# Attention over grouped heads: output rows of four pairs regrouped by 0/1 matmuls before the store

## The chip, the cores and the metric

The kernel runs on one core of a Trainium2 chip. The metric is the device time of one execution in microseconds. A core has TensorE (PE, with its weight loads shown as PEld), VectorE (DVE), ScalarE (ACT), GpSimd (POOL) and SyncE (SP), each with its own instruction stream; they wait for one another by semaphores. SP issues all DMA transfers here, into one queue that the core's 16 DMA engines work off together: each transfer is split evenly over the 16, and its semaphore tells of its landing when all 16 are done.

## The reference

```python
B, Hq, Hkv, Sq, Sk, D = 16, 32, 8, 16, 2048, 128       # q, k, v in bf16
k = jnp.repeat(k, Hq // Hkv, axis=1)
v = jnp.repeat(v, Hq // Hkv, axis=1)
scores = jnp.einsum("bhqd,bhkd->bhqk", q, k) * D ** -0.5
p = softmax(scores, axis=-1)
return jnp.einsum("bhqk,bhkd->bhqd", p, v)
```

K and V are 67 MB each, q and the output 2.1 MB each.

## The kernel before, in words

Four query heads share one head of K and V: 4 x 16 = 64 query rows for each of 128 groups. Two groups make a *pair* (128 query rows), and the kernel goes through NP = 64 pairs. A pair loads 1 MB of K (`Kn`, 6 buffers, 8192 bytes in a row on each partition) and 1 MB of V (`Vb`, 8 buffers, rows of 4096 bytes). Q is loaded four pairs at once, a *chunk* of 128 KB whose partition a holds the four rows 4a to 4a+3 (`load_q`, L202): 1024 bytes in a row.

For pair p the engines do this:

- DVE transposes K in two halves (`kt`, L343, KT<-Kn), always two pairs ahead.
- PE multiplies Q with the transposed K in tiles of 32 rows and 64 columns (op "S", L274 and L233). The scores have one PSUM tensor, `S_ps`, so S(p+1) waits until DVE has read those of pair p.
- DVE scales the scores into `Sneg` and takes the row minimum of the negated scores (L361); later it takes 1/rowsum (`recip`, L352).
- ACT computes exp with the row sums (op "exp", L391), PE transposes P in two halves (op "PT", L285), ACT moves each half out of PSUM (op "pe", L401).
- PE multiplies with V (op "PV", L302) three steps later (PVLAG = 3), and ACT scales the result into one of eight buffers `Osb` in bf16 (op "norm", L411).
- POOL copies each chunk of Q four times side by side (L176), PE transposes it (op "QT", L252), and ACT moves that out (op "qe", L381), in two parts in the first two steps of a chunk.

The orders of PE and ACT are two lists written out ahead (`pe_prog`, `act_prog`, L93 to L142). Step p holds on PE: S(p+1), PV(p-3), PT(p), and QT in two of four steps; on ACT: exp(p), norm(p-3), the two "pe", and "qe". DVE's order in step p is Sneg(p), recip(p-1), kt(p+2). A PSUM bank (`ST_ps`, third bank) is kept for the Q transposes (`stage_ap`, L153). PE's list runs as a loop over eight pairs, with steps 4 to 59 in it; the others are written out in full.

SP's order is one loop over t (L215): load K(t); a chunk of Q where it is due; load V(t-5) (VLAG); store pair t-12 (SLAG). Each load waits for its buffer: K(t) for `kt` of pair t-6, V(p) for PV(p-8). The V of the last pair comes in three pieces (CUTS), so that its PV can start early. A pair's store (`store`, L210) waits for its norm and moves 32 KB, 256 bytes from each partition, in the order of the output's rows; norm(p) in turn waits for the store of pair p-8, whose buffer it uses.

At the start POOL makes an iota and two identity matrices (L167 to L170, `sem_id`), and PE waits for these (L230).

Of the kernel before, what the change touches and what calls it, by code (L numbers as in the profile page):

```python
# [6 lines left out]
ALU = mybir.AluOpType  # L7
# [12 lines left out]
VLAG = 5  # L20
PVLAG = 3
SLAG = 12
QLEAD = 7
CUTS = (0, 8, 13, 16)


def bass_standalone__gqa_softmax__sampling_kernel(
# [12 lines left out]
    J = Sk // 128  # L40
    assert J == 16 and NP % BODY == 0 and BODY % (2 * QPAIRS) == 0
    NQC = NP // QPAIRS
    scale = float(D) ** -0.5

    ctx = ExitStack()
# [16 lines left out]
    nbias = sb("nbias", [128, NP], F32)  # L62
    rowsum = sb("rowsum", [128, NP], F32)
    rrec = sb("rrec", [128, NP], F32)

    S_ps = ctx.enter_context(nc.psum_tensor("S_ps", [128, Sk], F32))
    ST_ps = ctx.enter_context(nc.psum_tensor("ST_ps", [128, 3 * 512], F32))
# [5 lines left out]
    sem_vl = [sem(f"sem_vl{i}") for i in range(len(CUTS) - 1)]  # L73
    sem_q = [sem(f"sem_q{i}") for i in range(NQ)]
    sem_o = [sem(f"sem_o{i}") for i in range(NO)]
    sem_kt = sem("sem_kt")
    sem_q4 = sem("sem_q4")
    sem_max = sem("sem_max")
# [17 lines left out]
    def stage(*what):  # L96
        stages.append(what)
        return len(stages) - 1
# [22 lines left out]
    for p in range(NP - 1):  # L121
        step_at[p] = len(pe_prog)
        pe_prog.append(("S", p + 1))
        act_prog.append(("exp", p))
        if p >= PVLAG:
            pv(p - PVLAG)
            norm(p - PVLAG)
        transposes(p)
        c, i = divmod(p, QPAIRS)
        if c + 1 < NQC and i < 2:  # L130
            q_part(c + 1, i)
    tail_at = len(pe_prog)
    for p in range(NP - 4, NP - 2):
        pv(p)
# [6 lines left out]
    pv(NP - 1)  # L141
    norm(NP - 1)  # L142
    last_q = {what[1:]: u for u, what in enumerate(stages) if what[0] == "Q"}
    last_p = {what[1:]: u for u, what in enumerate(stages) if what[0] == "P"}

    first = PVLAG + 1
# [16 lines left out]
    with nc.Block() as block:  # L163

        @block.gpsimd
        def _(gp):
            gp.iota(iota_t[:, :], [[1, 128]], base=0, channel_multiplier=-1).then_inc(sem_id, 1)  # L167
            gp.wait_ge(sem_id, 1)
            gp.tensor_scalar(ident[:, :], iota_t[:, :], 0.0, None, op0=ALU.is_equal).then_inc(sem_id, 1)
            gp.tensor_scalar(ident4[:, :], iota_t[:, :], 0.0, None, op0=ALU.is_equal).then_inc(sem_id, 1)  # L170
            for c in range(NQC):
                gp.wait_ge(sem_q[c % NQ], 16 * (c // NQ + 1))
                if c >= 1:
                    gp.wait_ge(sem_st, last_q[c - 1, 1] + 1)
                src = Qn[c % NQ][:, :, :].rearrange("p j (b x) -> p (j b) x", b=2)
                gp.tensor_copy(  # L176
                    Q4[:, :, :, :, :].rearrange("p j b r x -> p (j b) r x"),
                    src.unsqueeze(2).to_broadcast([128, 2 * QPAIRS, 4, 64]),
                ).then_inc(sem_q4, 1)

        @block.sync
        def _(sp):
            def load_k(p):
                s = p % NK
                if p >= NK:
                    sp.wait_ge(sem_kt, p - NK + 1)
                sp.dma_start(Kn[s][:, :], kf[p]).then_inc(sem_k[s], 16)  # L187

            def load_v(p):
                s = p % NV  # L190
                if p >= NV:
                    sp.wait_ge(sem_pv, p - NV + 1)
                if p < NP - 1:
                    dst = Vb[s][:, :, :, :].rearrange("a g j d -> a g (j d)")
                    sp.dma_start(dst, vf[:, 2 * p:2 * p + 2, :]).then_inc(sem_v[s], 16)  # L195
                    return
                for x, (lo, hi) in enumerate(zip(CUTS, CUTS[1:])):
                    dst = Vb[s][:, :, lo:hi, :].rearrange("a g j d -> a g (j d)")
                    src = vf[:, 2 * p:2 * p + 2, D * lo:D * hi]
                    sp.dma_start(dst, src).then_inc(sem_vl[x], 16)  # L200

            def load_q(c):  # L202
                s = c % NQ
                if c >= NQ:
                    sp.wait_ge(sem_q4, c - NQ + 1)
                rows = 128 * QPAIRS
                src = qf[rows * c:rows * (c + 1), :].rearrange("(a j) d -> a j d", j=QPAIRS)
                sp.dma_start(Qn[s][:, :, :], src).then_inc(sem_q[s], 16)

            def store(p):  # L210
                s = p % NO
                sp.wait_ge(sem_nm, p + 1)
                sp.dma_start(of[128 * p:128 * (p + 1), :], Osb[s][:, :]).then_inc(sem_o[s], 16)  # L213

            for t in range(NP + SLAG + 1):  # L215
# [12 lines left out]
        @block.tensor  # L228
        def _(pe):
            pe.wait_ge(sem_id, 3)  # L230

            def matmul_on_loaded(out, lhsT, rhs, tile, start, stop):
                return pe.add_instruction(mybir.InstMatmult(  # L233
# [7 lines left out]
            def emit(op, at, v_at):  # L241
# [36 lines left out]
                elif op[0] == "PT":  # L278
                    _, p, h, u = op
                    if h == 0:  # L280
                        pe.wait_ge(sem_exp, at(p + 1))
                    dst = stage_ap(("P", p, h))
                    for t in range(4):
                        x = 4 * h + t
                        ins = pe.transpose(dst[:, 128 * t:128 * (t + 1)], P[p % 2][:, 128 * x:128 * (x + 1)], ident4[:, :])  # L285
                    ins.then_inc(sem_st, 1)
                elif op[0] == "PV":
                    _, p = op
                    if p >= NP - 4:
                        pe.wait_ge(sem_ev, last_p[p, 1] + 1)  # L290
                    if p < NP - 1:
                        pe.wait_ge(sem_v[p % NV], v_at(p))
                    if p == NP - 3:
                        pe.wait_ge(sem_max, NP)
                    elif 1 <= p < NP - 3:
                        pe.wait_ge(sem_nm, at(p))
                    pt = PT[p % NPT][:, :, :].bitcast(BF16).rearrange("p t (q e) -> p t e q", e=2)
                    for j in range(J):
                        if p == NP - 1 and j in CUTS:
                            pe.wait_ge(sem_vl[CUTS.index(j)], 16)  # L300
                        for g in range(2):
                            ins = pe.matmul(  # L302
                                o_ap(p)[64 * g:64 * (g + 1), :],
                                pt[:, j // 2, j % 2, 64 * g:64 * (g + 1)],
                                Vb[p % NV][:, g, j, :],
                                start=(j == 0), stop=(j == J - 1),
                                skip_group_check=True,
                            )
                    ins.then_inc(sem_pv, 1)
# [64 lines left out]
        def _(act):  # L374
            for op in act_prog:
# [9 lines left out]
                elif op[0] == "exp":  # L385
                    _, p = op
                    act.wait_ge(sem_max, p + 1)
                    if p >= 2:
                        act.wait_ge(sem_st, last_p[p - 2, 1] + 1)

                    act.activation(  # L391
                        P[p % 2][:, :].bitcast(BF16).rearrange("p (n y e) -> p n y e", n=16, e=2),
                        Sneg[p % 2][:, :].rearrange("p (n e y) -> p n y e", n=16, e=2), ACT.Exp,
                        bias=nbias[:, p:p + 1], scale=-1.0, accum_out=rowsum[:, p:p + 1],
                    ).then_inc(sem_exp, 1)
                elif op[0] == "pe":
                    _, p, h, u = op
                    act.wait_ge(sem_st, u + 1)
                    if h == 0 and p >= NPT:
                        act.wait_ge(sem_pv, p - NPT + 1)  # L400
                    act.activation(  # L401
                        PT[p % NPT][:, 4 * h:4 * (h + 1), :].rearrange("p t q -> p (t q)"),
                        stage_ap(("P", p, h)), ACT.Copy,
                    ).then_inc(sem_ev, 1)
                else:
                    _, p = op
                    act.wait_ge(sem_pv, p + 1)
                    act.wait_ge(sem_rec, p + 1)
                    if p >= NO:
                        act.wait_ge(sem_o[p % NO], 16 * (p // NO))  # L410
                    act.activation(Osb[p % NO][:, :], o_ap(p), ACT.Copy,  # L411
                                   scale=rrec[:, p:p + 1]).then_inc(sem_nm, 1)

# [27 lines left out]
```

## Time and profile before

| | |
|---|---|
| median of three runs | 341.72 us (341.66 to 341.79) |
| profiled execution: whole / span on the core | 342.24 us / 340.5 us |
| granted TensorE clock, mean | 0.993 |
| read from HBM / written | 136.31 MB / 2.10 MB |
| mean rate over the span | 407 GB/s |
| DMA packets: all / under 512 B / under 2 KB | 38705 / 11552 / 14112 |
| Sneg (L361), 64 times | 2.26 us each |
| exp (L391), 64 times | 2.49 us each |
| half a K transpose (L343), 128 times | 1.22 us each |
| norm (L411), 61 times | 0.37 us each |

The span runs from the first instruction of the program to the last one on the core; the whole execution adds what lies around it. The profile counts an engine as busy when it works on data, not when it issues DMAs or waits. Under 512 bytes there are 8192 packets of 256 bytes (64 stores of 128 packets); nearly all others are the 4-byte packets that end a transfer on each of the 16 DMA engines. In the chain of work that ended last, "DMA Vb<-in_v_dram" is the time from issue to landing of a V load, its place in the queue included.

### The profile page before, as it was taken

Reading aid. Unit: us, or ns where it says so; the run is one execution under the profiler, and the core shown is the slowest. Engines: PE = TensorE matmul, PEld = TensorE weight load, DVE = VectorE, ACT = ScalarE, POOL = GpSimd, SP = SyncE. Lnnn points to the kernel's source line nnn. Section 1 sums busy time; section 2 is a strip of 40 time slices with the busy share of each in tenths; the row PEclk is TensorE's granted clock in tenths of the full one; section 3 lists DMA queues with packets and bytes.
Section 4 is the critical chain, followed back from the end, with each engine's and each line's share of the span. In section 5 each row is a group of like instructions: output and inputs, shape, how many; then the busy total and the mean of one; then the engine's idle time right before and its main releaser. Section 6 shows DMA issues by size and latency. Waiting matters only on the chain.

```text
span 340.5 us, 9888 instructions
## 1 busy us (share of the span) xinstructions
PE 278.8 (82%) x4736; PEld 161.6 (47%) x3712; DVE 295.3 (87%) x320; ACT 267.0 (78%) x353; POOL 31.8 (9%) x23
## 2 busy tenths in 40 slices
PE   0687999999998787888788797897878878888885
PEld 0233555555465445445355354454454454454454
DVE  2489999999999988989989889889889889899860
ACT  1178889999888786877878877887878869778785
POOL 3202020202010020200202011020200202000000
PEclk9979999999999999999999999999999999999999
DMA  8999999999999999999999999999999999999996
GB/s 295 398 418 416 410 414 409 414 415 415 416 418 415 416 417 417 415 419 417 416 418 412 420 418 413 420 416 417 420 413 418 414 416 420 419 415 420 416 409 205
DMA packets 38705, 138.63 MB, mean 407 GB/s; under 512 B 11552, under 2 KB 14112, under 8 KB 30496
## 3 DMA queue, kind: packets, MB, share of 16 engines
q1 hardware_dynamic: 38688, 138.43, 100.7%
q8 instruction: 8, 0.13, 0.2%
q14 instruction: 9, 0.07, 0.1%
HBM read 136.31 MB, written 2.10 MB: 407 GB/s over the span
## 4 chain that ended last, share of the span: by engine, by line
DMA 58%; DVE 16%; SPq 10%; issue 7%; PE 6%; ACT 1%; POOL 1%
DMA Vb<-in_v_dram 52%; DVE KT L343 11%; SPq L187 7%; DVE Sneg L361 5%; DMA Kn<-in_k_dram 5%; PE O_ps L302 3%; SPq L213 2%; DMA Qn<-in_q_dram 1%; ACT O L411 1%; PE S_ps L274 1%; PE S_ps L233 1%; SPq L195 1%; PE ST_ps L252 1%; POOL Q L176 1%; SPq L200 0%
## 5 line engine op out<-in xcount | busy, mean ns | idle before, releaser
L343 DVE STREAM_TRANSPOSE KT<-Kn 128x1024 f32<-128x1024 f32 x128 | 151.5, 1222 | 28.7 <-DMA Kn<-in_k_dram 28.7
L391 ACT ACTIVATE P<-Sneg,nbias 128x2048 bf16<-128x2048 f32 x64 | 159.6, 2493 | 6.0 <-DVE Sneg L361 6.0
L361 DVE TENSOR_SCALAR_CACHE_REDUCE Sneg<-S_ps 128x2048 f32<-128x2048 f32 x64 | 144.4, 2256 | 7.1 <-PE S_ps L233 7.1
L274 PE MATMUL S_ps<-KT,QT 32*64 32x512 bf16 x1024 | 105.7, 393 | 6.7 <-DVE Sneg L361 5.1
L233 PE MATMUL S_ps<-KT,QT 32*64 32x512 bf16 x1024 | 104.8, 388 | 0.0
L302 PE MATMUL O_ps<-Vb,PT 128*64 128x128 bf16 x1952 | 66.2, 221 | 38.0 <-DMA Vb<-in_v_dram 38.0
L302 PEld LDWEIGHTS O_ps<-Vb,PT 128*64 128x64 bf16 x1952 | 56.5, 110 | 80.4 <-issue 43.5
L401 ACT ACTIVATE PT<-ST_ps 128x512 f32<-128x512 f32 x128 | 69.5, 595 | 19.2 <-PE ST_ps L285 19.2
L285 PE MATMUL ST_ps<-ident,P 128*128 128x128 f32 x512 | 70.5, 281 | 4.7 <-ACT P L391 4.3
L274 PEld LDWEIGHTS S_ps<-KT,QT 32*64 32x64 bf16 x1024 | 32.4, 104 | 71.0 <-issue 60.3
L285 PEld LDWEIGHTS ST_ps<-ident,P 128*128 128x128 f32 x512 | 55.3, 141 | 13.9 <-ACT P L391 9.6
L176 POOL COPY Q<-Qn 128x2048 bf16<-128x2048 bf16 x16 | 30.3, 1893 | 255.9 <-PE ST_ps L252 252.0
L411 ACT ACTIVATE O<-O_ps,rrec 128x128 bf16<-128x128 f32 x61 | 22.5, 369 | 35.1 <-PE O_ps L302 35.0
L252 PE MATMUL ST_ps<-ident,Q 128*128 128x128 f32 x128 | 20.2, 282 | 8.8 <-POOL Q L176 8.1
L381 ACT ACTIVATE QT<-ST_ps 128x512 f32<-128x512 f32 x32 | 19.3, 603 | 8.5 <-PE ST_ps L252 8.5
L252 PEld LDWEIGHTS ST_ps<-ident,Q 128*128 128x128 f32 x128 | 15.5, 145 | 9.2 <-issue 8.1
L391 ACT ACTIVATION_READ_ACCUMULATOR P<-Sneg,nbias 128x1 f32 x64 | 13.2, 207 | 0.0
L352 DVE RECIPROCAL rrec<-rowsum 128x1 f32<-128x1 f32 x64 | 10.2, 159 | 3.0 <-ACT P L391 3.0
L361 DVE DVE_READ_ACCUMULATOR Sneg<-S_ps 128x1 f32 x64 | 5.3, 84 | 0.0
L302 PE MATMUL S_ps<-Vb,PT 128*64 128x128 bf16 x96 | 3.6, 221 | 1.1 <-issue 0.6
L302 PEld LDWEIGHTS S_ps<-Vb,PT 128*64 128x64 bf16 x96 | 2.9, 110 | 1.9 <-issue 1.5
L411 ACT ACTIVATE O<-S_ps,rrec 128x128 bf16<-128x128 f32 x3 | 1.1, 369 | 2.0 <-PE S_ps L302 2.0
(8 smaller groups left out, 3.0 us busy)
## 6 DMA issues: line engine op xcount, KB each, us to landing
Kn<-in_k_dram SPq DMA_DIRECT2D x64, 1024.0 KB, 15.9
Vb<-in_v_dram SPq DMA_DIRECT2D x63, 1024.0 KB, 16.4
Qn<-in_q_dram SPq DMA_DIRECT2D x16, 128.0 KB, 15.5
out_dram<-O SPq DMA_DIRECT2D x64, 32.0 KB, 15.4
Vb<-in_v_dram SPq DMA_DIRECT2D x1, 512.0 KB, 12.6
Vb<-in_v_dram SPq DMA_DIRECT2D x1, 320.0 KB, 12.3
Vb<-in_v_dram SPq DMA_DIRECT2D x1, 192.0 KB, 12.4
```

The lines of the kernel that those rows point to most:

```text
L176: gp.tensor_copy(Q4[:, :, :, :, :].rearrange("p j b r x -> p (j b) r x"), src.unsqueeze(2).to_broadcast([128, 2 * QPAIRS, 4, 64]),).then_i ...
L187: sp.dma_start(Kn[s][:, :], kf[p]).then_inc(sem_k[s], 16)
L233: return pe.add_instruction(mybir.InstMatmult(name=nc.get_next_instruction_name(), engine=mybir.EngineType.PE, ins=[pe.lower_ap(rhs), pe.l ...
L252: ins = pe.transpose(dst[:, 128 * j:128 * (j + 1)], src[:, j, b, :], ident4[:, :])
L274: ins = pe.matmul(s_ap, w, x, start=(acc == 0), stop=(acc == 3))
L285: ins = pe.transpose(dst[:, 128 * t:128 * (t + 1)], P[p % 2][:, 128 * x:128 * (x + 1)], ident4[:, :])
L302: ins = pe.matmul(o_ap(p)[64 * g:64 * (g + 1), :], pt[:, j // 2, j % 2, 64 * g:64 * (g + 1)], Vb[p % NV][:, g, j, :], start=(j == 0), stop ...
L343: ins = dve.transpose(KT[p % NKT][:, :].rearrange("p (t b e a x) -> p x e t b a", t=J // 2, b=2, e=2, x=2)[:, x, :, :, :, :], Kn[p % NK][: ...
L361: dve.tensor_scalar(Sneg[p % 2][:, :].rearrange("p (t h x) -> p h t x", t=8, h=2), S_ps[:, :].rearrange("p (h t x) -> p h t x", t=8, h=2), ...
L391: act.activation(P[p % 2][:, :].bitcast(BF16).rearrange("p (n y e) -> p n y e", n=16, e=2), Sneg[p % 2][:, :].rearrange("p (n e y) -> p n ...
L401: act.activation(PT[p % NPT][:, 4 * h:4 * (h + 1), :].rearrange("p t q -> p (t q)"), stage_ap(("P", p, h)), ACT.Copy,).then_inc(sem_ev, 1)
L411: act.activation(Osb[p % NO][:, :], o_ap(p), ACT.Copy, scale=rrec[:, p:p + 1]).then_inc(sem_nm, 1)
```

## The change

The outputs of pairs 0 to 55 are no longer stored pair by pair. Four pairs make a chunk, as with Q; there are NRC = 14 such chunks, and the last eight pairs keep the store that they had.

- A constant `sel` of 0 and 1 is made by POOL with a further iota and a compare: sel[p, j, a] is 1 where p = 4a + j. PE's first wait, and so everything on PE, is now for these as well (`sem_id` 5 in place of 3).
- A new PE op "R" for chunk c, placed at the end of step p = 4c + 7 (RLAG = 7), multiplies for each pair x of the chunk and each j the `Osb` of that pair by sel[:, j, :]: 16 matmuls with 128 x 32 weights and 128 columns. Row 4a + j of pair x comes to partition 32x + a, columns 128j to 128j + 127. The result fills the PSUM bank that the Q transposes use.
- A new ACT op "re", at the end of the same step, moves the 128 x 512 values out of PSUM into one of four buffers `Rsb` in bf16. From chunk 4 on it waits for the store of four chunks before.
- SP stores chunk c at t = 4c + 18 (RSLAG = 18): 128 KB, 1024 bytes from each partition, which are one run of the output. It waits for "re". The pair's own store remains for pairs 56 to 63, at t = p + 12 as before.
- norm no longer waits for an earlier store of its buffer.

`sel` and `Rsb` are allocated after all other buffers in SBUF, so that these keep their places.

```diff
+RLAG = 7
+RSLAG = 18
+NR = 4
...
+    NRC = NP // QPAIRS - 2
...
+    sel = sb("sel", [128, QPAIRS, 32], BF16)
+    Rsb = [sb(f"R{i}", [128, QPAIRS, 128], BF16) for i in range(NR)]
...
             q_part(c + 1, i)
+        c, i = divmod(p - RLAG, QPAIRS)
+        if i == 0 and 0 <= c < NRC:
+            u = stage("R", c)
+            pe_prog.append(("R", c))
+            act_prog.append(("re", c, u))
...
+            gp.wait_ge(sem_id, 3)
+            gp.iota(iota_t[:, :], [[1, QPAIRS], [QPAIRS, 32]], base=0, channel_multiplier=-1).then_inc(sem_id, 1)
+            gp.wait_ge(sem_id, 4)
+            gp.tensor_scalar(sel[:, :, :].rearrange("p j a -> p (j a)"), iota_t[:, :], 0.0, None,
+                             op0=ALU.is_equal).then_inc(sem_id, 1)
...
+            def store_chunk(c):
+                sp.wait_ge(sem_ev, last_r[c] + 1)
+                dst = of[128 * QPAIRS * c:128 * QPAIRS * (c + 1), :].rearrange("(a j) d -> a j d", j=QPAIRS)
+                sp.dma_start(dst, Rsb[c % NR][:, :, :]).then_inc(sem_r[c % NR], 16)
...
-                if 0 <= t - SLAG < NP:
+                c, i = divmod(t - RSLAG, QPAIRS)
+                if i == 0 and 0 <= c < NRC:
+                    store_chunk(c)
+                if NRC * QPAIRS <= t - SLAG < NP:
                     store(t - SLAG)
+            for s in range(NR):
+                sp.wait_ge(sem_r[s], 16 * ((NRC - s + NR - 1) // NR))
             for s in range(NO):
-                sp.wait_ge(sem_o[s], 16 * (NP // NO))
+                sp.wait_ge(sem_o[s], 16)
...
-            pe.wait_ge(sem_id, 3)
+            pe.wait_ge(sem_id, 5)
...
+                elif op[0] == "R":
+                    _, c = op
+                    for x in range(QPAIRS):
+                        for j in range(QPAIRS):
+                            ins = pe.matmul(
+                                stage_ap(op)[32 * x:32 * (x + 1), 128 * j:128 * (j + 1)],
+                                sel[:, j, :], Osb[(QPAIRS * c + x) % NO][:, :], start=True, stop=True,
+                            )
+                    ins.then_inc(sem_st, 1)
...
+                elif op[0] == "re":
+                    _, c, u = op
+                    act.wait_ge(sem_st, u + 1)
+                    if c >= NR:
+                        act.wait_ge(sem_r[c % NR], 16 * (c // NR))
+                    act.activation(
+                        Rsb[c % NR][:, :, :].rearrange("a j d -> a (j d)"), stage_ap(op), ACT.Copy,
+                    ).then_inc(sem_ev, 1)
...
-                    if p >= NO:
-                        act.wait_ge(sem_o[p % NO], 16 * (p // NO))
```

More of the change, by code (lines that the diff above doesn't have):

```diff
@@ L75, in bass_standalone__gqa_softmax__sampling_kernel @@
     sem_o = [sem(f"sem_o{i}") for i in range(NO)]
+    sem_r = [sem(f"sem_r{i}") for i in range(NR)]
     sem_kt = sem("sem_kt")
@@ L143, in bass_standalone__gqa_softmax__sampling_kernel @@
     last_q = {what[1:]: u for u, what in enumerate(stages) if what[0] == "Q"}
+    last_r = {what[1]: u for u, what in enumerate(stages) if what[0] == "R"}
     last_p = {what[1:]: u for u, what in enumerate(stages) if what[0] == "P"}
```

## The prediction

> **What bounds the kernel now.** I read the page first (busy shares, DMA row, queues, chain, issues). Five of its parts carry the answer:
>
> ```profile
> PE 278.8 (82%) x4736; PEld 161.6 (47%) x3712; DVE 295.3 (87%) x320; ACT 267.0 (78%) x353; POOL 31.8 (9%) x23
> ...
> DMA  8999999999999999999999999999999999999996
> ...
> q1 hardware_dynamic: 38688, 138.43, 100.7%
> ...
> DMA 58%; DVE 16%; SPq 10%; issue 7%; PE 6%; ACT 1%; POOL 1%
> ...
> Kn<-in_k_dram SPq DMA_DIRECT2D x64, 1024.0 KB, 15.9
> Vb<-in_v_dram SPq DMA_DIRECT2D x63, 1024.0 KB, 16.4
> Qn<-in_q_dram SPq DMA_DIRECT2D x16, 128.0 KB, 15.5
> out_dram<-O SPq DMA_DIRECT2D x64, 32.0 KB, 15.4
> ```
>
> No compute engine is full, but the one DMA queue is busy in every slice, and whatever its size a transfer lands 15 to 16 us after its issue: that is queueing. Then the waits between 100 and 320 us (who waits for whom: us, times, longest):
>
> ```profile
> PE O_ps L302 <- DMA Vb<-in_v_dram: 37.0, 42, 1.4
> ...
> ACT O L411 <- PE O_ps L302: 32.0, 41, 1.4
> DVE KT L343 <- DMA Kn<-in_k_dram: 21.7, 41, 0.9
> ```
>
> In nearly every pair both PE and DVE stand still until a load lands. The kernel is bound by the time that its 16 DMA engines need for the packets in the queue. The queue's own waits name ACT O (71.4 us) before the stores; this I set aside: the store that starts at 139.60 is number 18, whose norm was done at 119.5, so SP waits for room in a full queue.
>
> **Price of a packet.** The trace has a record for each packet. Records of one engine overlap by a few ns (DMA share 1.03 in the table of stretches), so I use the distance from start to start on one engine, in the steady stretch (80 to 300 us; my sorting of the records into 16 engines):
>
> | packet | in | record, ns | start to start, ns |
> |---|---|---|---|
> | 256 B | store of O | 18 | 14.0 |
> | 1024 B | load of Q | 46 | 42.3 |
> | 4096 B | load of V | 161 | 157.8 |
> | 8192 B | load of K | 309 | 306.2 |
> | 4 B | end of each DMA | 9 | 6 |
>
> On each engine a store is 8 x 14.0 + 6 = 118 ns, a Q load 8 x 42.3 + 6 = 344, K 8 x 306.2 + 6 = 2456, V 16 x 157.8 + 6 = 2531. Four pairs and one Q: 4 x (2456 + 2531 + 118) + 344 = 20.76 us. The timeline shows the same: two K transposes that each start as their K lands, four pairs apart, lie 20.70 us apart.
>
> ```profile
> 141.15 2.37 DVE L343 STREAM_TRANSPOSE KT<-Kn 128x1024 f32<-128x1024 f32 x2 [0.45 <-DMA Kn<-in_k_dram]
> ...
> 161.85 2.37 DVE L343 STREAM_TRANSPOSE KT<-Kn 128x1024 f32<-128x1024 f32 x2 [0.47 <-DMA Kn<-in_k_dram]
> ```
>
> **The change, part by part.** *Stores removed.* Pairs 0 to 55 lose their own store; all 56 stood in SP's order ahead of the last V load (t = 68, with store 55 at t = 67): 56 x 118 = 6.61 us less on each engine before that load lands.
>
> *Chunk stores added.* Of 14, chunks 0 to 12 are issued by t = 66, before the last V load. No row shows a store of 1024-byte packets. From below: no row moves more than 8192 B in 306.2 ns, so 1024 B need 38.2 ns, the chunk 8 x 38.2 + 6 = 312. From above: four packets of 256 B, 32 x 14.0 + 6 = 454. I take the Q load of equal shape, 344, because the 256-B store already lies on the loads' line (5 ns and 37 ns a KB give 14). 13 x 344 = 4.47 us; the ends give 4.06 and 5.90.
>
> *Sum on the DMA engines:* 6.61 - 4.47 = **2.14 us earlier** landing of the last V (2.55 to 0.71).
>
> *R on PE and "re" on ACT, 14 times.* R is 16 matmuls of 128x32 weights over 128 columns. Nearest rows: P.V (64 columns wide, two side by side), 32 in 1.09 us, 34 ns each; the f32 transposes, 137 ns each. So 0.5 to 2.2 us; R's four matmuls of one x share a column group and follow each other, so I take two P.V slots, 68 ns, 1.1 us. "re" has the form of L401, 0.6 us. R stands between PT(p) and S(p+2), p = 3 mod 4. Queued behind it on PE is S(p+2), for which DVE's Sneg waits; behind "re" on ACT is exp(p+1), for which PT(p+1) waits. In series that is up to 1.7 us in four pairs (2.8 at the dear end). Cover: PE waits for V 37.0 us in the 220 us shown, 42.7 pairs, so 3.5 us in four pairs, and ACT's 32.0 stands behind the same wait; DVE waits for K 21.7 / 42.7 x 4 = 2.0 us in four, and S of such a pair ends about 0.7 us before Sneg can start (151.14 to 153.2 against 153.97), so a delay of 1.1 reaches DVE as 0.4. Walking it on: Sneg is 0.4 late, the next kt 0.1, and the next wait for V has swallowed the rest. Cost 0. Without this cover the price is 14 x 1.7 = 24 us. From 18 to 93 us DVE is the chain (4.53 us a pair) and three or four R delay it by about 1 us each, but then 5 to 8 MB lie in the queue, so the DMA engines don't notice.
>
> *SP.* 42 issues fewer; chunk store c is issued at t = 4c+18 and waits for "re" of step 4c+7; K(t) can go out only after kt(t-6) of step t-8, so SP is at step 4c+10 at the earliest. No wait. "re" waits for the chunk store four chunks back, issued three steps or more before and 16 us in the queue: landed two or more steps ahead. ACT's wait per norm for a store goes; it never ended last.
>
> *Start.* Two more POOL instructions before PE may begin, like these (0.23 + 0.53 us):
>
> ```profile
> 1.65 0.53 POOL L170 TENSOR_SCALAR ident<-iota_t 128x128 f32<-128x128 int32 x1
> ...
> 6.10 1.89 POOL L176 COPY Q<-Qn 128x2048 bf16<-128x2048 bf16 x1 [3.93 <-DMA Qn<-in_q_dram]
> ```
>
> POOL is then done at about 3.1 us and still waits for Q until 6.05. Cost 0; uncovered 0.9.
>
> *The end.*
>
> ```profile
> 335.17 1.08 PE L302 MATMUL S_ps<-Vb,PT 128*64 128x128 bf16 x32
> 336.30 0.37 ACT L411 ACTIVATE O<-S_ps,rrec 128x128 bf16<-128x128 f32 x1 [0.53 <-PE S_ps L302]
> ...
> 336.56 1.56 PE L302 MATMUL S_ps<-Vb,PT 128*64 128x128 bf16 x32 [0.31 <-DMA Vb<-in_v_dram]
> ```
>
> The last pair's P.V starts 0.31 us late and takes 1.56 us instead of 1.08, since V comes in pieces: compute alone would have ended some 0.8 us sooner. The V that released that chain (V58) has 51 stores and 12 chunks ahead: it moves 51 x 118 - 12 x 344 = 1.89 us. Compute is late by 2.14 - 1.89 = 0.25 against 0.8 of slack, so the last V still ends last. Behind it lie seven stores (0.17 us each, landing 337.90 to 338.93) and now chunk 13: 1.55 us, while the last store's packets start 1.66 us after V. Cost 0, but barely.
>
> **Sum.** The profiled execution took 342.24 us (span 340.5 and 1.7 around it); less 2.14, 340.1. It lies 0.5 above the median of the runs, 341.72, so the forecast for the median is **339.6 us**.
>
> [...] In the timeline PE goes from P.V (64 columns) to the transposes (128) to S (32x64 tiles) with no gap over 0.1 us. [...] Code: queue q8 fetched 16 KB six times between 27 and 75 us (about 1.05 us on one engine), then none until 328, so PE's loop stays held. [...]
>
> **Rivals.** (1) *Slower: stores ran in the loads' shadow.* Between 26 and 40 us, without stores, 413 GB/s: 5.08 us for a pair's 2.10 MB; from 275 to 315 us, with them, 418 GB/s: 5.10 us for 2.13 MB. Read so, a store cost 20 ns, not 118, while a chunk may cost Q's full 344: 13 x 344 - 56 x 20 = +3.4 us, 345.1. It decides below 80 ns a store (13 x 344 / 56). Against it: the early K records are longer (314 to 318 ns against 309), and the steady slots add up to the measured 20.7 with nothing hidden. 0.10. (2) *The R step is not covered*, by its dear end and ACT's 0.6 beside the Q steps: the gain is eaten, 341.0 to 343, about 341.7. Against: 3.5 us of waits. 0.10. (3) *One more code fetch on the slowest engine* (engines land up to 3 us apart; the last one counts): +1.05, 340.7. 0.12. (4) *Packets stay 256 B:* 13 x 454, 341.0; Q's same pattern on both sides gives 1024. 0.04. Forecast: 0.64.
>
> **Range.** The forecast's own bounds are 339.2 to 341.0; a fetch that leaves the slowest engine instead takes 1.05 off (338.2 at the low end). 338.3 to 341.3 leaves out rival 1 and half of rival 2, and a little below. A measurement can tell 0.2%, 0.7 us. Faster: 0.64 + 0.12 and half of rival 4, less a remainder, 0.75; slower: rival 1 and a third of rival 2, 0.13; within: the rest, 0.12.
>
> **What would show it.** Right: 1024-B store records near 46 ns; four-pair distance of K transposes near 20.6; waits for V and K still there in 100 to 320; R about 1.1 us. Wrong: waits for K and V gone, with PE or ACT ahead of Sneg (rival 2); chunk stores over 500 ns in the queue, or K records shorter than 306 beside them (rival 1); q8 fetches during the loop.

## The result and the profile after

The change makes the kernel slower, not faster: 342.70 us (median of ten runs, 342.64 to 343.99) against 341.76 us (ten runs, 341.30 to 341.92). The ratio is 1.0033, with a 95% interval of 1.0024 to 1.0042. The forecast was 339.6 us (338.3 to 341.3).

The page of the profiled execution after (whole 342.7 us), in the lines that answer to those of before:

```profile
span 340.9 us, 10322 instructions
...
PE 284.8 (84%) x4960; PEld 164.8 (48%) x3936; DVE 295.7 (87%) x320; ACT 273.2 (80%) x367; POOL 32.6 (10%) x25
...
DMA  7999999999999999999999999999999999999996
...
q1 hardware_dynamic: 32640, 138.42, 100.3%
q8 instruction: 8, 0.13, 0.2%
...
DMA 59%; ACT 18%; PE 9%; issue 6%; DVE 4%; SPq 3%; POOL 1%
...
Kn<-in_k_dram SPq DMA_DIRECT2D x64, 1024.0 KB, 19.5
Vb<-in_v_dram SPq DMA_DIRECT2D x63, 1024.0 KB, 19.5
...
out_dram<-R SPq DMA_DIRECT2D x14, 128.0 KB, 18.7
```

The change does what it says: 6,048 packets fewer in q1 for the same bytes, and 14 stores of 128 KB. Yet the share of time that the queue's packets took is nearly what it was (100.3% against 100.7%), in a span that is 0.4 us longer. With so many packets gone, the ones that stayed must each have taken longer. The DMA engines are still busy in every slice, and a transfer now waits longer in the queue (19.5 us against 16).

The waits between 100 and 320 us after (who waits for whom: us, times, longest):

```profile
PE O_ps L339 <- DMA Vb<-in_v_dram: 29.5, 37, 1.9
...
ACT O L454 <- PE O_ps L339: 24.8, 35, 1.9
DVE KT L380 <- DMA Kn<-in_k_dram: 20.2, 36, 1.0
```

These are the three rows of before, all shorter (37.0, 32.0 and 21.7 us there), and no wait for another engine has taken their place. The kernel is still bound by its loads.

The timeline after, with the two K transposes four pairs apart and one R step between them:

```profile
150.75 2.38 DVE L380 STREAM_TRANSPOSE KT<-Kn 128x1024 f32<-128x1024 f32 x2 [0.77 <-DMA Kn<-in_k_dram]
...
171.20 0.44 PE L319 MATMUL ST_ps<-O,sel 128*32 128x128 bf16 x16
...
171.57 2.37 DVE L380 STREAM_TRANSPOSE KT<-Kn 128x1024 f32<-128x1024 f32 x2 [0.75 <-DMA Kn<-in_k_dram]
...
171.84 0.60 ACT L447 ACTIVATE R<-ST_ps 128x512 bf16<-128x512 f32 x1
```

Each transpose starts as its K lands (the bracket). They lie 20.82 us apart, where before had 20.70 and the forecast 20.6. A finer measure of the same thing is used from here on: the moment at which a V load has landed, as the mean over its 16 engines, taken for the V of pair 16 and of pair 56 and divided by ten (my sorting of the trace's landing records). Between these two lie 40 pairs with all their stores, but only eight of the Q chunks. It gives 20.703 us for four pairs before and 20.771 after. The difference, 0.0686 us before rounding, times the 14 groups of four pairs that changed, is 0.96 us, as much as the loss of 0.94 us between the medians: it lies in the steady stretch. (The two profiled executions themselves differ by less, 342.24 and 342.70 us, since that of before lies 0.5 above its median: its V of pair 16 landed at 105.62 us, after's at 105.12.)

The stretches view from 100 to 290 us (window, length, busy us of PE, PEld, DVE, ACT, POOL, granted clock, DMA share, GB/s), first before, then after:

```profile
100.00:290.00 190.00, 157.41 (x2736) 91.16 (x2143) 171.04 (x186) 153.63 (x204) 18.93 (x10) 1.00 1.03 417
```

```profile
100.00:290.00 190.00, 162.14 (x2906) 94.52 (x2310) 172.11 (x186) 159.10 (x215) 18.96 (x10) 1.00 1.02 415
```

Clock and DMA share are alike; the rate fell by 2 GB/s, although the packets became larger.

### The profile page after: what moved, and what is told of

It is laid out like the page before. It is cut to its first block, busy times and chain, and to the rows that moved or that the text cites. A ratio compares the mean times of both kernels' runs of the same rounds, so it can differ in the third digit from the quotient of the medians.

```text
span 340.9 us, 10322 instructions
## 1 busy us (share of the span) xinstructions
PE 284.8 (84%) x4960; PEld 164.8 (48%) x3936; DVE 295.7 (87%) x320; ACT 273.2 (80%) x367; POOL 32.6 (10%) x25
## 3 DMA queue, kind: packets, MB, share of 16 engines
q1 hardware_dynamic: 32640, 138.42, 100.3%
## 4 chain that ended last, share of the span: by engine, by line
DMA 59%; ACT 18%; PE 9%; issue 6%; DVE 4%; SPq 3%; POOL 1%
DMA Vb<-in_v_dram 39%; DMA Kn<-in_k_dram 19%; ACT P L428 13%; ACT PT L438 4%; PE ST_ps L313 4%; DVE KT L380 3%; PE S_ps L302 2%; DVE Sneg L398 2%; PE S_ps L261 2%; DMA Qn<-in_q_dram 1%; SPq L218 1%; PE O_ps L339 1%; SPq L205 1%; PE ST_ps L280 1%; POOL Q L194 1%
## 5 line engine op out<-in xcount | busy, mean ns | idle before, releaser
L302 PEld LDWEIGHTS S_ps<-KT,QT 32*64 32x64 bf16 x1024 | 31.7, 104 | 70.5 <-issue 58.8
L447 ACT ACTIVATE R<-ST_ps 128x512 bf16<-128x512 f32 x14 | 8.4, 603 | 0.0
L319 PE MATMUL ST_ps<-O,sel 128*32 128x128 bf16 x224 | 6.1, 222 | 0.0
L319 PEld LDWEIGHTS ST_ps<-O,sel 128*32 128x32 bf16 x224 | 3.7, 95 | 2.3 <-issue 2.3
## 6 DMA issues: line engine op xcount, KB each, us to landing
Kn<-in_k_dram SPq DMA_DIRECT2D x64, 1024.0 KB, 19.5
Vb<-in_v_dram SPq DMA_DIRECT2D x63, 1024.0 KB, 19.5
Vb<-in_v_dram SPq DMA_DIRECT2D x1, 512.0 KB, 15.9
```

The source lines that it names most:

```text
L302: ins = pe.matmul(s_ap, w, x, start=(acc == 0), stop=(acc == 3))
```

## The experiments

All times are medians. Runs that were made together share the runs of the kernel before; its median was 341.76 to 341.87 us each time. The theories that the expectations name are these. **A**: the loads of all 16 engines together can't go faster than about 20.50 us for four pairs, and each engine by itself not faster than its own packets; a store that lies between costs only what doesn't fit in the gap. **B**: every store, whatever its size, hides a fixed 60 to 70 ns. **C**: the deeper queue of after (19.5 us instead of 16) makes the packets longer. A further rival was that the R step itself delays the loads. **D** came later: a load packet without a store beside it simply has a higher price. The first expectations use other letters: T1 is a shadow in which stores hide, T2 is the depth of C, T3 is the R step.

### No stores at all, without and with R

`b_nostore` is the kernel before without the stores of pairs 0 to 55:

```diff
-                if 0 <= t - SLAG < NP:
+                if NP - NO <= t - SLAG < NP:
...
-                    if p >= NO:
-                        act.wait_ge(sem_o[p % NO], 16 * (p // NO))
```

> The kernel before without the stores of pairs 0 to 55, and without norm's waits for them (those outputs are not written). Three theories for the change's +0.9 us. T1, shadow: loads run faster while a small store lies among them, so that 56 stores cost far less than their 56 x 118 ns; expected 339 to 341, 1 to 3 us under the kernel before, with K packets at 309 ns from start to start instead of 306. T2, depth: with fewer store descriptors the queue holds more bytes (a load lands 19.5 us after its issue in the changed kernel, 16 before) and a deeper queue is slower; this run is deep as well, so loads are slow: the same 339 to 341. T3, R and re: packets cost what was forecast and the matmuls eat it; expected 335.1 (341.7 - 6.6), K packets at 306.

`a_nostore` is the kernel after without its 14 chunk stores; R and "re" are kept:

```diff
-                if i == 0 and 0 <= c < NRC:
-                    store_chunk(c)
```

> The changed kernel without its 14 chunk stores; R and re stay, their result is left in the buffers (the outputs of pairs 0 to 55 are not written). T1 and T2: R and re cost nothing, so the time is that of the kernel before without stores, within 0.5 us, and the chunk stores cost what lies between this and 342.7 (14 x 344 ns = 4.8 by their packets: 337.9; less where they too run in the shadow). T3: it stays 1.5 us or more above the kernel before without stores.

Measured: 339.19 us (ratio 0.9922, 0.9909 to 0.9936) and 339.39 us (0.9925, 0.9912 to 0.9939). So the change can be taken apart: without the 56 small stores the kernel gains 2.65 us, R and "re" cost 0.20 (no more than these runs scatter), and the 14 chunk stores cost 3.31. A small store costs 47 ns (2.65 / 56), not its slot of 118; a chunk store costs 236 ns (3.31 / 14), not its slot of 344. Both are partly hidden, but the small ones far better. R's delay is not the cause: four pairs take 20.502 us in the one and 20.504 in the other.

The same stretch of `b_nostore`:

```profile
100.00:290.00 190.00, 159.43 (x2765) 91.91 (x2162) 172.34 (x189) 155.34 (x207) 18.93 (x10) 1.00 1.02 414
```

The reader is to see the 414. The queue holds nothing but loads, and still it moves fewer bytes per second than before with its small packets (417). The load packets themselves have become slower. My sorting of the records between 100 and 300 us by whether a store's packet is in flight on any of the 16 engines as they start shows it for the K packets (8192 bytes):

| kernel | no store in flight | beside a store |
|---|---|---|
| before | 309.6 ns | 309.2 ns |
| after | 314.3 | 309.2 |
| no stores | 315.3 | - |

In these runs a K packet had a floor of 309 ns (306 from start to start), which it kept as long as stores lay close by, and took some 5 to 6 ns more where nothing but loads ran. In before the K packets stayed at the floor even when no store was in flight, because the relief outlasted the store and the next one was never far off there. The records of after show how long: the K packets that start within 1.25 us of the end of a chunk store's last packet have 309.0 to 309.2 ns, those that start more than 2 us behind it some 315. In `b_burst` (below), with four small stores in a row, it lasts some 3 us. The share of K packets at the floor (records up to 311 ns) is 18% without stores, 39% after, 94% before.

### The chunk store in parts

`a_split` cuts the chunk store into four of 32 partitions, one a step; `a_split2` into two of 64; `a_split8` into eight of 16, one behind each K and one behind each V. The packets remain 1024 bytes. The core of the edit, here for eight:

```diff
-                sp.dma_start(dst, Rsb[c % NR][:, :, :]).then_inc(sem_r[c % NR], 16)
+                h = 128 // 8
...
+                sp.dma_start(dst, Rsb[c % NR][h * x:h * (x + 1), :, :]).then_inc(sem_r[c % NR], 16)
...
+                if 0 <= c < NRC:
+                    store_part(c, 2 * i)
...
-                if i == 0 and 0 <= c < NRC:
-                    store_chunk(c)
+                if 0 <= c < NRC:
+                    store_part(c, 2 * i + 1)
```

> The changed kernel with each chunk store cut in four, one a step, 32 partitions of 1024 bytes each (2 packets on each DMA engine): same bytes, same packets, spread like the stores before. T1, if the shadow belongs to each store and not to its bytes: these 91 ns are hidden as the 118 ns were, 339.5 to 341.0. T1, if it is shared by bytes: 342 to 342.7. T2: the queue is as deep as in the changed kernel or deeper, so no better than it, 342.5 to 343. T3: 342.7 or more.

> The changed kernel with each chunk store cut in two halves of 64 partitions, two steps apart. So far, for four pairs (mean landing of V over the 16 engines): no stores 20.50 us, four small ones 20.70, four parts of 1024-byte packets 20.69, one chunk 20.77, four small ones in a row 20.84. Theory A, two limits: all loads together can't go faster than 20.50 (shared), each engine by itself not faster than its own packets (4 x 4.95 + 0.34 for Q + its stores); a store is free as far as the other engines can use the time meanwhile, so spreading helps only down to the engine's own sum. Here 350 ns of stores in two pieces: between one and four pieces, 20.71 to 20.75, 341.9 to 342.4. Theory B, each store event hides 60 to 70 ns whatever its size: 350 - 135, 20.71, 342.0. Theory C, queue depth: 342.7.

> The changed kernel with each chunk store cut in eight parts of 16 partitions, one packet of 1024 bytes on each engine, two a step (behind K and behind V). Theory A: 388 ns of stores, engine's own sum 20.53, so nearly all can be hidden: 20.58 to 20.65, 340.2 to 341.2. Theory B: 48 ns hide completely, 20.50, 339.2 to 339.6. Theory C: no better than the changed kernel, 342.7.

Measured: 341.63 us in four parts (0.9994, 0.9985 to 1.0003), 341.92 in two (1.0010, 1.0001 to 1.0019), 342.06 in eight (1.0009, 1.0000 to 1.0018). Four pairs take 20.693, 20.729 and 20.590 us, against 20.771 for the chunk in one piece. The same bytes in the same packets cost less here, the more the pieces were spread, and the share of K packets at the floor rises from 39% in one piece to 53% in two and 74% in four (73% in eight). `a_split` met none of its ranges; `a_split2` and, for four pairs, `a_split8` lie where theory A put them. In the steady stretch eight parts are the best; the total lost it at the end, as the timeline of `a_split8` shows (norm of the last pair, and SP's issues of stores):

```profile
334.43 0.89 SPq L234 DMA_DIRECT2D out_dram<-R  x2
335.37 0.42 SPq L239 DMA_DIRECT2D out_dram<-O  x1
335.83 0.89 SPq L234 DMA_DIRECT2D out_dram<-R  x2
336.77 1.37 SPq L239 DMA_DIRECT2D out_dram<-O  x3
...
336.58 0.37 ACT L460 ACTIVATE O<-S_ps,rrec 128x128 bf16<-128x128 f32 x1 [1.35 <-PE S_ps L345]
```

The last norm ends at 336.95, but SP takes some 0.45 us for each issue there (0.42 for one, 0.89 for two) and is still at work on the parts of the last chunks, so the last store goes out late; the span ends at 340.3, 4.2 us after the last V landed (336.13). Before, these were 2.7 us apart.

### Small stores in a row, and in halves

`b_burst` is the kernel before with 16 output buffers; its small stores go out four in a row, at the chunk's place. `b_half` cuts each pair's store into two of 64 rows, one behind K and one behind V.

```diff
+                c, i = divmod(t - RSLAG, QPAIRS)
+                if i == 0 and 0 <= c < NQC - 2:
+                    for x in range(QPAIRS):
+                        store(QPAIRS * c + x)
```

> The kernel before with 16 buffers for O, in which the four 256-byte stores of pairs 4c to 4c+3 are issued one behind the other at t = 4c + 18, where the changed kernel has its chunk store; no R, no re. T1 with a shadow for each store: the four are one event, most of 472 ns shows, 14 x 0.25 to 0.3: 345 to 346. T1 by bytes: 341.7. T2: as many descriptors as before and the same depth, 341.7. T3: 341.7.

```diff
+                if 0 <= t - SLAG < NP:
+                    store(t - SLAG, 0)
...
-                    store(t - SLAG)
+                    store(t - SLAG, 1)
```

> The kernel before with each pair's store cut in two halves of 64 partitions (four packets of 256 bytes on each engine), one behind K and one behind V. Theory A: the engine's own sum is the bound already (4 x 4.95 + 0.34 + 0.50 = 20.64), so spreading brings nothing: 20.68 to 20.75, 341.6 to 342.3. Theory B: all is hidden, 20.50, 339.2 to 339.6. Theory C: more descriptors, queue less deep, 341.8 or less.

Measured: `b_burst` 343.42 us (1.0045, 1.0032 to 1.0059), 20.837 us for four pairs; `b_half` 342.75 us (1.0030, 1.0018 to 1.0041), but 20.622 for four pairs. The burst has the packets of before and the place of after, and it is the slowest of the four (before, after, burst and halves): with the same packets the place alone costs 1.6 us. Neither range for it held (345 to 346, 341.7). The halves put more packets in the queue than before and are faster in the steady stretch, and lose it in the tail in the same way as the eight parts. Theory B, by which each piece hides its own 60 to 70 ns, would have halves hide everything (20.50); it falls. Theory A had expected no gain from halves (20.68 to 20.75), which does not hold either.

### Depth of the queue

`a_nk3` is the kernel after, whose K load waits for the transpose of three pairs before instead of six.

```diff
-                if p >= NK:
-                    sp.wait_ge(sem_kt, p - NK + 1)
+                if p >= 3:
+                    sp.wait_ge(sem_kt, p - 3 + 1)
```

> The changed kernel in which the load of K waits for the transposes of the pair three before instead of six, so that fewer bytes lie in the queue than in the kernel before (landing under 14 us after issue); buffers and work are the same. Theory A and B: depth has no part in it, 20.77 for four pairs, 342.5 to 343.0 (more if the queue runs dry). Theory C: loads as fast as in the kernel before, K packets at 306 ns, 20.6 to 20.7, 341 or less.

The time, 349.41 us (1.0227, 1.0209 to 1.0245), says nothing on the theory by itself, since the queue ran dry early on (`a_nk3`, rate by slice, and its issues between 100 and 300 us with the median us to landing):

```profile
GB/s 294 348 224 355 413 411 413 413 411 418 411 419 413 418 411 420 415 411 420 408 419 416 413 417 415 417 413 418 417 411 422 411 416 416 416 418 416 415 410 213
...
Kn<-in_k_dram SPq DMA_DIRECT2D x38, 1024.0 KB, 13.2
```

From the fifth slice on it is comparable: a K load lands 13.2 us after its issue, less than before (15.9) and after (20.4 in this window), a V load 15.3 (16.4 and 19.5), and four pairs still take 20.767 us. `b_burst` has before's depth and is slower than after:

```profile
Kn<-in_k_dram SPq DMA_DIRECT2D x40, 1024.0 KB, 16.0
```

Theory C falls.

### Spread stores with the tail left whole

The last eight pairs' stores, or the last two chunks, remain in one piece, so that SP has nothing more to issue at the end than before. `b_half_t` and `b_quarter_t` cut the small stores of before in two and in four; `a_split8_t` cuts the first 12 chunks in eight.

```diff
+                if 0 <= c < NRC - 2:
+                    store_part(c, 2 * i)
...
+                if 0 <= c < NRC - 2:
+                    store_part(c, 2 * i + 1)
+                elif i == 0 and 0 <= c < NRC:
+                    store_chunk(c)
```

> The kernel before with the stores of pairs 0 to 55 cut in two halves (one behind K, one behind V), and those of the last eight pairs whole, so that SP has eight DMAs less to issue at the end. Without the last point the four pairs took 20.62 us, and the last V landed 1.1 us earlier than before, but the last store went out 2.0 us after the last norm had ended, behind other issues on SP. Theory A (two limits) with the end now free: span 339.0 to 339.5, time 340.3 to 341.0. If the end is not SP's issues but the slots of the DMA engines, it stays at 342 or above.

> The kernel before with the stores of pairs 0 to 55 cut in four parts of 32 partitions (two behind K, two behind V; two packets of 256 bytes on each engine), the last eight whole. Theory A: the engine's own sum goes from 20.64 to 20.68, and that is the bound: 0.04 to 0.08 per four pairs above the halves, 20.66 to 20.72, time 0.5 to 1.1 above the halved stores. If only the spread counts: the same as the halves or better, 20.5 to 20.6.

> The changed kernel with chunks 0 to 11 in eight parts of 16 partitions, and chunks 12 and 13 whole. With all 14 in parts four pairs took 20.59 us and the last V landed at 336.1, but SP issued the last store 0.8 us after the last norm, behind other issues, and the last eight landed 0.2 to 0.6 us apart. Theory A with the end free: last V at 336.2 to 336.6, span 338.5 to 339.3, time 340.2 to 341.1, level with the halved pair stores or up to 0.5 better. If R's packets matter beyond that, 339.5.

Measured: 341.24 us (0.9984, 0.9975 to 0.9993), 341.49 us (0.9991, 0.9982 to 1.0000) and 340.74 us (0.9971, 0.9961 to 0.9982). `a_split8_t` beats both kernels: 1.06 us under before, 1.96 under after, within its range; `b_half_t` stayed 0.24 us above the range of theory A, and `b_quarter_t` took 20.643 us for four pairs, outside both of its ranges. SP's part of its timeline:

```profile
329.00 1.21 SPq L231 DMA_DIRECT2D out_dram<-R  x1
330.26 7.00 SPq L244 DMA_DIRECT2D out_dram<-O  x6
```

SP is through with the chunks by 330.2 and then waits for the norms, one issue each. The last V lands at 336.08, as in `a_split8`, but the span ends at 338.8 instead of 340.3.

### Is it a limit on loads, or the packet's price?

Theory A and its rival D both allow what was seen so far. Two runs cut each V load in two, with rows of 2048 bytes: same bytes, more time on each engine.

```diff
-                    dst = Vb[s][:, :, :, :].rearrange("a g j d -> a g (j d)")
-                    sp.dma_start(dst, vf[:, 2 * p:2 * p + 2, :]).then_inc(sem_v[s], 16)
+                    for lo in (0, J // 2):
+                        dst = Vb[s][:, :, lo:lo + J // 2, :].rearrange("a g j d -> a g (j d)")
+                        src = vf[:, 2 * p:2 * p + 2, D * lo:D * (lo + J // 2)]
+                        sp.dma_start(dst, src).then_inc(sem_v[s], 16)
```

> The kernel before without the stores of pairs 0 to 55 (these outputs are left out, as in the run without stores), and each V load but the last pair's cut into two DMAs whose rows are 2048 bytes instead of 4096. By the line through the slots of 1024, 4096 and 8192 bytes (about 5 ns and 37 ns a KB) a 2048-byte packet takes some 80 ns alone on one engine, so V by itself costs some 80 ns more a pair on each engine, +0.31 us per four pairs. Theory A (the loads of all 16 engines together share a limit of 20.50 us per four pairs, and each engine alone could do it in 20.14): the own sum rises to 20.45, still under the shared limit, so most of it disappears: 20.52 to 20.65 per four pairs, 339.5 to 341.4 us against the 339.2 without the cut. Rival D (no shared limit: a packet without a store beside it is simply longer, 310 and 159 ns, and the sum on each engine is the time): the whole 0.31 shows, 20.8 per four pairs, +4.5 to +5, about 344 us.

> The kernel before, with all stores, and each V load but the last pair's cut into two DMAs whose rows are 2048 bytes. Theory A: with its stores (0.47 us per four pairs) each engine's own sum becomes 20.14 + 0.31 + 0.47 = 20.92, above the shared limit of 20.50, so now the engines themselves decide and stores cost nearly their full slot: 20.90 to 21.0 per four pairs, +3 to +4.5 us, 344.7 to 346.2; a store then costs over 90 ns (the difference from the run of the same loads without stores, 4 us or more, over 56). Rival D (lengthened packets, no shared limit): a small store costs what it did, 47 ns, the difference from the same loads without stores stays 2.6 us, about 346.5 with that run at 344.

Measured: 348.91 us without stores (1.0209, 1.0195 to 1.0223) and 351.12 with them (1.0278, 1.0264 to 1.0292); four pairs take 21.117 and 21.267 us. Both theories expected less. If the loads had a common limit of 20.50 us, the first run would have stayed near it, since its engines' own floor (20.38, see the table) is below that; instead it went up by 0.61 us. So the runs show no fixed limit of bytes per time, and A is wrong in that form. D falls short as well: the cut cost twice the 0.31 us that it gave. And the K records, whose packets were left as they are, went from 315.3 to 317.6 ns when V was cut, so a load packet's length was not a price of its own alone here: what was loaded beside it had a part in it. What did hold is that a store costs little: (351.12 - 348.91) / 56 = 39 ns. In this run, too, the load packets are longer than their floor (2048 bytes: 80 ns at the 10th percentile, 83.7 in the mean), and less so with stores.

The stretches view of `b_nostore_v2k`, for comparison with the 414 of `b_nostore`:

```profile
100.00:290.00 190.00, 152.64 (x2626) 88.45 (x2052) 165.10 (x180) 147.72 (x197) 17.04 (x9) 0.99 1.04 403
```

### Other places in HBM

The last two runs read the K and V of pair 0 over and over, without and with the stores:

```diff
-                sp.dma_start(Kn[s][:, :], kf[p]).then_inc(sem_k[s], 16)
+                sp.dma_start(Kn[s][:, :], kf[0]).then_inc(sem_k[s], 16)
...
-                    sp.dma_start(dst, vf[:, 2 * p:2 * p + 2, :]).then_inc(sem_v[s], 16)
+                    sp.dma_start(dst, vf[:, 0:2, :]).then_inc(sem_v[s], 16)
```

> The kernel before without the stores of pairs 0 to 55, and every K load reads the K of pair 0, every V load but the last pair's the V of pair 0 (so the outputs are those of other data, and most are left out). Buffers, sizes, order and waits are the same; only the places read in HBM are. If the stretch of the load packets (K 311 ns from start to start against 306 at the floor, V 159.4 against 155) comes of where the rows lie in HBM, it changes: down to the floor would be 20.1 us per four pairs, about 333.5 us; it could also grow. If it comes of the core's side (the 16 engines, what they write into SBUF), nothing changes: 20.50 per four pairs, 339.2 us within 0.5.

> The kernel before with all its stores, K and V always read from pair 0 as in the run beside it (the outputs are those of other data). If the stretch stays (core's side), a store still costs 47 ns: 341.8 us, 2.6 above the run beside it. If the stretch goes (HBM's side), a store has nothing left to hide in and costs nearly its 118 ns: 6 us or so above the run beside it, about 339.5 to 340.

Measured: 339.21 us (0.9924, 0.9911 to 0.9938) and 341.89 us (1.0000, 0.9990 to 1.0009), the same as with all of K and V (339.19 and 341.8); four pairs take 20.503 and 20.715 us. Which rows of HBM were read played no part. The stretches view of `b_nostore_one` has the 414 again:

```profile
100.00:290.00 190.00, 158.70 (x2761) 91.60 (x2156) 171.88 (x186) 154.73 (x206) 18.86 (x10) 1.00 1.02 414
```

### The runs side by side

For each kernel the floors of its packets can be added up: 306 ns for 8192 bytes, 155 for 4096, 80 for 2048 (10th percentile of the distance from start to start between 100 and 300 us, the same in all kernels but for a nanosecond), 42.3 for 1024, 14.0 for 256, and 6 for the packet that ends a transfer. Before: 4 x (8 x 306 + 6 + 16 x 155 + 6) = 19.76 us for K and V, 0.8 x 0.344 = 0.276 for Q (eight chunks in ten groups), 4 x 118 ns of stores, 20.508 in all. What was measured beyond it is the **stretch**. Kernels whose transfers are of the same sizes and places agree within 0.012 us in the measured column (before and `b_one`, after and `a_nk3`, the three without stores), so differences of a few hundredths count.

| kernel | pieces of stores in four pairs | floors, us | measured, us | stretch, us | time, us |
|---|---|---|---|---|---|
| no stores (`b_nostore`) | 0 | 20.036 | 20.502 | 0.47 | 339.19 |
| after | 1 x 128 KB | 20.380 | 20.771 | 0.39 | 342.70 |
| `a_nk3` | 1 x 128 KB | 20.380 | 20.767 | 0.39 | 349.41 |
| `a_split2` | 2 x 64 KB | 20.386 | 20.729 | 0.34 | 341.92 |
| `b_burst` | 4 x 32 KB in a row, 256-byte packets | 20.508 | 20.837 | 0.33 | 343.42 |
| `a_split` | 4 x 32 KB | 20.398 | 20.693 | 0.30 | 341.63 |
| before | 4 x 32 KB, 256-byte packets | 20.508 | 20.703 | 0.20 | 341.76 |
| `a_split8_t` | 8 x 16 KB | 20.422 | 20.586 | 0.16 | 340.74 |
| `b_half_t` | 8 x 16 KB, 256-byte packets | 20.532 | 20.615 | 0.08 | 341.24 |
| `b_quarter_t` | 16 x 8 KB, 256-byte packets | 20.580 | 20.643 | 0.06 | 341.49 |
| `b_nostore_v2k` | 0 | 20.380 | 21.117 | 0.74 | 348.91 |
| `b_v2k` | 4 x 32 KB, 256-byte packets | 20.852 | 21.267 | 0.42 | 351.12 |

The stretch belongs to the loads, and in the kernels with uncut V loads it went down with every place at which stores were interspersed, from 0.47 us with none to 0.06 with 16; the stores' own floors go on top. At the same number of places the 256-byte packets leave less stretch (0.20 against 0.30, 0.08 against 0.16), about as much less as their floors are higher (0.11). The change traded 0.13 us less of floors (0.472 of small stores against 0.344 of a chunk) for 0.20 us more of stretch (0.20 to 0.39, rounded). The difference, 0.07 us in four pairs, is the result. In the two runs without stores the stretch is about the same for each load packet, not for each byte: 0.466 us over 96 packets of K and V on each engine is 4.9 ns, 0.737 us over 160 is 4.6 (estimates from the table).

## Why the prediction was wrong

**The step that failed** is "Price of a packet", and with it the "Sum on the DMA engines". It read from the trace of before how far apart the packets of each kind start (306.2 ns for K, 157.8 for V) and took these as prices that stay when the stores go. They are not: without the small stores K went to 309.7 ns and V to 159.0 in after, and to about 311 and 159.4 with no stores at all. 8 x 3.5 + 16 x 1.2 = 47 ns more a pair is 0.19 us in four pairs, more than the 0.128 (0.472 - 0.344) that the forecast had counted as gain. So "56 x 118 = 6.61 us" was really 2.65, and "13 x 344 = 4.47 us" was really 3.31 for 14. Both were too high, but by factors of 0.40 and of about 0.7, and it is the difference that makes the sign.

**"The steady slots add up to the measured 20.7 with nothing hidden"** was the argument against rival 1, and it was empty: slots that were measured with the stores in place add up to the time with the stores in place, whatever they hide. The second argument, that "the early K records are longer (314 to 318 ns against 309)", spoke for the rival: between 26 and 40 us there were no stores, and the longer records were the stretch itself.

**Rival 1 was right in its mechanism** and in its point of decision: a store costs less than 80 ns (47 measured), so the change loses. Its sizes were off on both sides, since it put the store at 20 ns and let the chunk cost its full 344 (236 measured): +3.4 us instead of +0.94. The sign that it named in the profile, "K records shorter than 306 beside them", came in another form: K's records beside the chunk stores are at the floor (309.2 ns), and the others rose to 314.3. Its other sign, chunk stores over 500 ns, did not come: their slot is 344.

**What held.** The 1024-byte packets of the store have records of 46 ns and slots of 42.3 to 42.6, as the Q load had. The cover for R held: the waits for V and K are still there, and R and "re" cost 0.20 us (`a_nostore` against `b_nostore`), within the scatter of those runs. R itself takes 0.44 us and not the 1.1 that was chosen, even less than the forecast's cheap end; the waits had room for either. That R's matmuls of one x share a column group and so take two P.V slots, 68 ns, was the author's estimate, and no run shows it: the 16 took 28 ns each (0.44 us / 16). POOL was done with `sel` at 3.11 us (forecast 3.1) and then still waited 2.88 us for Q; PE began at 8.02 us (8.14 before). Code was fetched in 8 packets of q8 as before (six between 27.7 and 73.7 us, then none until 325.8), so rival 3 did not come, and the store's packets are of 1024 bytes, so rival 4 did not either. In the tail the last V still ends last, 2.7 us ahead of the end of the span in both kernels (337.72 and 340.47 before, 338.15 and 340.89 after).

**R's tile shape and the size of the stores.** For R's change of tile shape the trace shows a price of 0.2 us at most: R's 16 matmuls take 0.44 us and follow the transposes without a gap; behind R the next matmul follows without a gap in eight of the 14 cases and after 0.15 to 0.20 us in six, for which the profile names no releaser. Nor was one large store cheaper here than several small ones: 12 chunks cut into stores of 16 KB are 1.96 us faster than in stores of 128 KB (340.74 against 342.70 us). The change was decided by the stretch above the floors.

**What stays open** is why the loads stretched one another when nothing but loads ran. It is not the depth of the queue (20.767 us for four pairs in `a_nk3` against 20.771 in after), not the R step (20.504 against 20.502), not the rows of HBM that are read (20.503 against 20.502), and not a fixed limit of bytes per time (21.117 against 20.502); smaller load packets made it worse (0.74 us in four pairs against 0.47), for K packets that did not change too (317.6 ns against 315.3). Whether it comes up on the way into SBUF, among the 16 engines or in HBM whatever the place was not tried.

## What to carry to other kernels

A slot read from a trace is the price of a packet among its present neighbours (here 306.2 ns from start to start for a K packet in before, and about 311 with no stores); before a saving on one kind of packet is booked, look in the same trace for a stretch without that kind (here 26 to 40 us, with K records of 314 to 318 ns against 309) and see whether the others get slower there. In this queue, full of loads, stores were best cut fine and spread between the loads (20.586 us for four pairs with eight pieces, 20.771 with one); with that done, larger packets gained a little more (eight pieces in four pairs: 20.586 us with 1024-byte packets, 20.615 with 256-byte ones). At the end of the program it was the other way round: there every further issue took SP 0.42 to 0.46 us and nothing hid it (`a_split8` 342.06 us, `a_split8_t` 340.74).

## What the runs showed of the hardware

The 16 DMA engines shared each transfer evenly (each of the 168 in after has 16 landing records and 16 of the 4-byte packets that end a transfer, and slots added up with even shares gave 20.76 us for four pairs of before, 20.703 measured) but did not keep in step: the last engine landed 0.7 to 2.6 us after the mean of the 16 (V of pairs 16 to 56, all traces; 1.4 to 2.1 in before, 1.1 to 1.9 in after), so times of two executions differed by some tenths of a us without a cause in their steady stretch (`a_nostore` and `b_nostore` as profiled, at 340.03 and 339.19 us: the last V landed at 335.20 and 334.62 with the same 20.50 us for four pairs). Loads alone reached 8.49 MB / 20.502 us = 414 GB/s here, and with finely spread stores the total was higher (the stretches view of `a_split8` gives 419), so finely spread stores added to what the engines moved. One issue of a store took SP 0.42 to 0.46 us at the end of `a_split8`.
